# Moving the softmax steps of a fused FFT and soft mixture-of-experts kernel to other places in its written order

## The chip, the cores and the metric

The kernel runs on one core of one Trainium2 chip. The metric is the device time in microseconds (us) of one execution. The engines are named as in the profile: PE (TensorE, matmuls and transposes), PEld (its weight loads), DVE (VectorE), ACT (ScalarE), POOL (GpSimd) and SP (SyncE, which issues all the DMAs here).

## What is computed

The input x is 8 batches of 2496 x 256 float32. The real part of its 2-D Fourier transform, reshaped to 19968 tokens of 256, goes into a soft mixture of experts with 8 experts of 4 slots each:

```python
x = np.fft.fft(np.fft.fft(x, axis=1), axis=2).real.reshape(B * S, D)   # 19968 x 256
logits = x @ phi                                    # 19968 x 32
d = softmax(logits, axis=0)                         # over all tokens
slot_input = (d.T @ x).reshape(8, 4, 256)
slot_out[e] = np.maximum(slot_input[e] @ w1[e], 0.0) @ w2[e]
c = softmax(logits, axis=1)                         # over the 32 slots
out = c @ slot_out                                  # 19968 x 256
```

Both softmaxes subtract the maximum first and add 1e-9 to the sum.

## The kernel before

The 8 batches are worked on as 4 pairs. The transform is never written out: phi is transformed instead, so the first part of the program (parts a to e, d, u) computes the logits of each pair and the sums over tokens. Part m combines the pairs' sums to the experts' input. Parts l and v are the experts: l is h = relu(slot input x w1), in two groups of 32 matmuls (l00, l10), with the relu on ACT (hs) and a transpose on DVE (hT); v is the second matmul (so), also in two groups (v00, v10). Part r copies the experts' output to a replicated matrix rh, by an ACT copy (sos), one matmul (sorep) and two ACT scalings. Everything after this writes the output.

The softmax over slots belongs to each pair and has six steps, named x in the order with the pair and the step:

- x_0, `logits`: 11 transposes of the pair's logits on PE (cT), in groups of 4, 4 and 3, each group copied by ACT to the tile c. The two PSUM banks with the tag p1 are shared by cT and lT.
- x_1, `less_max` for both halves: a max reduce on DVE and a subtraction on POOL each.
- x_2 and x_3, `exp` of one half each, on ACT.
- x_4 and x_5, `over_sum` of one half each: sum reduce, small scaling (adding 1e-9) and reciprocal on DVE, then a multiplication on POOL.

Part s is all six steps of one pair at once. Part k (k00 to k32) transposes a piece of a finished softmax on PE (lT) and copies it with ACT (lTs). Pieces 0, 1 and 2 serve the output blocks 0 and 1, 2 and 3, and 4. Part o is an output block: 8 matmuls as the profile counts them (po, against rh) in two halves, whose banks are emptied by one ACT copy and one DVE copy each (line 612), then a DMA on SP. There are 5 blocks for each of 4 pairs, 20.45 MB in all. Six PSUM banks serve po. The first block of the first pair is sent in three DMAs, the last block of a pair in two pieces.

The order is written by hand: `ORDER` is a list of parts with a pair and an index, and the parts are traced in that order. A planner then orders each engine's queue; it may put work that is ready earlier ahead. `after` holds it back: it queues what a part traces behind the last output matmul and the last output copies traced so far, each on its own engine, with no wait for their end. Where there are none yet, it takes the instruction in `anchor["u"]`, the last matmul of part u. `GATE` holds back the cT groups of pairs 0 and 1 in the same way on PE: for pair 1 behind `anchor["slot"]`, the last matmul of part m. `part_s` also holds its DVE work behind the copies of sT, the experts' input.

In the order before, the first pair's softmax stands between the experts' two groups of h (l00 s00 l10), the second's right after them (s10), ahead of v00. The third's and the fourth's six steps are spread over the output blocks of the first and second pair, from k01 to k11 and from o11 to o21.

Of the kernel before, what the change touches and what calls it, by code (L numbers as in the profile page):

```python
# [15 lines left out]
D = 256  # L16
# [11 lines left out]
SEB = 2  # L28
DE = 2
FIRST = [0, 1]  # L30
GATE = {0: ['u', 'acc', 'acc'], 1: ['slot', 'slot', 'slot']}
P1, P2, P3, PM = 2, 2, 3, 0
W2 = [1, 1, 1, 1, 1, 1, 1, 1, 1, 1, 1, 2, 2, 1]
ORDER = (
# [6 lines left out]
).split()  # L41


# [69 lines left out]
def _build(nc, tc, xh, phih, w1h, w2h, cins, where, out, out0):  # L113
    from contextlib import ExitStack, nullcontext

    v, sc, pe = nc.vector, nc.scalar, nc.tensor
    ctx = ExitStack()
    with ctx:
# [8 lines left out]
        def ring(name):  # L127
            return sb.tile([128, 8, D], F32, name=name, tag="ring", bufs=RING)
# [13 lines left out]
        def bank(name, dt=F32):  # L142
            return pp.tile([128, 512], dt, name=name, tag="ps")
# [31 lines left out]
        def C(name):  # L175
            i, o, r, w = where[name]
            return cs[i][:r, o : o + w]
# [5 lines left out]
        ps = bank("psphi")  # L183
# [238 lines left out]
        acc = cp.tile([128, 129], F32, name="acc")  # L422
        at = cp.tile([128, 64], F32, name="at")
        sT = cp.tile([128, 2, NSLOT], F32, name="sT")
        anchor = {}
# [79 lines left out]
        def part_r():  # L505
            so = sos_[0]

            rh.append(sb.tile([128, 2, D], F32, name="rh", tag="d", bufs=2))
            sos = sb.tile([128, D], F32, name="sos", tag="dpm", bufs=2)
            ps = bank("sorep")  # L510
            sc.copy(sos, so[:, :D])
            pe.matmul(ps[:, :D], C("sel2"), sos, start=True, stop=True)
            for k in range(2):
                sc.activation(rh[0][:, k], ps[:, :D], AF.Copy, scale=C("turn")[:, k : k + 1])  # L514
            banks.close()
            pool_o.append(ctx.enter_context(tc.tile_pool(name="po", bufs=6, space=PSUM)))
# [4 lines left out]
        def logits(p):  # L521
            L = lt[p]
            cq[p] = sb.tile([128, 40, NSLOT], F32, name=f"c{p}", tag=CT[p], bufs=bufs_(CT[p]))
            for b in range(3):
                ps = bank1(f"cT{p}_{b}")
                n = min(4, NG - 4 * b)
                with tc.issue_after(anchor[GATE[p][b]]) if p in GATE else nullcontext():
                    for j in range(n):
# [50 lines left out]
        behind, lts = {}, {}  # L579
# [12 lines left out]
            for t in range(n):  # L592
                lts[p, 2 * j + t // 2, t % 2] = lT[:, t]

        def part_o(p, b):
            ot = ring(f"o{p}_{b}")
            done = 0
            for t in range(2):

                po = [pool_o[0].tile([128, 512], F32, name=f"po{p}_{b}_{2 * t + h}", tag="po") for h in range(2)]  # L600
                for h in range(2):
                    rows = slice(64 * h, 64 * h + 64)
                    with tc.issue_after(behind["pe"]) if "pe" in behind else nullcontext():
                        ins = pe.matmul(  # L604
                            po[h], lts[p, b, t][rows], rh[0][rows].rearrange("p k d -> p (k d)"),
                            start=True, stop=True, tile_position=(64 * h, 0),
                        )
                    behind["pe"] = ins.ins
                for h, ev in ((0, sc.copy), (1, v.tensor_copy)):
                    i = 2 * t + h  # L610
                    np_ = 64 if b == 4 and i == 3 else 128
                    ins = ev(ot[:np_, 2 * i : 2 * i + 2, :].rearrange("p k d -> p (k d)"), po[h][:np_])  # L612
                    behind[h] = ins.ins
                    if b == 4 and i == 3:
                        nc.sync.dma_start(out0[p].rearrange("p (r d) -> p r d", d=D), ot[:64, 6:8])
                    elif i == 3 or (b == 4 and i == 2) or ((p, b) == (0, 0) and i in FIRST):
                        nc.sync.dma_start(
                            out[p, :, (8 * b + done) * D : (8 * b + 2 * i + 2) * D].rearrange("p (r d) -> p r d", d=D),
                            ot[:, done : 2 * i + 2],
                        )  # L620
                        done = 2 * i + 2

        def after(f, *a):

            with ExitStack() as order:
                for ins in behind.values() if behind else [anchor["u"]]:
                    order.enter_context(tc.issue_after(ins))
                f(*a)

# [2 lines left out]
            "e": part_e, "d": part_d, "u": lambda p, _: part_u(p), "w": lambda *_: load_w(),  # L632
            "m": lambda *_: part_m(), "l": lambda i, _: part_l(i), "v": lambda i, _: part_v(i),
            "r": lambda *_: part_r(), "s": lambda p, _: after(part_s, p), "x": lambda p, i: after(part_x, p, i),
            "k": lambda p, j: after(part_k, p, j), "o": part_o,
        }
        for what in ORDER:
            parts[what[0]](int(what[1]), int(what[2]))
# [50 lines left out]
```

## Time and profile before

| | |
|---|---|
| median of 3 runs | 198.22 us (197.83 to 199.21) |
| the profiled execution | 199.02 us |
| its span | 196.9 us |
| PE busy | 170.5 us, 87% of the span |
| DVE busy | 125.4 us, 64% |
| ACT busy | 111.2 us, 56% |
| POOL busy | 20.8 us, 11% |
| granted TensorE clock, mean | 0.982 |
| moved by DMA | 38.46 MB read, 20.45 MB written |

The profile shows one execution. The page gives each engine's busy time and cuts the span into 40 slices. Other views of the same trace are windows (busy time of each engine in a stretch, the number of instructions in brackets, then the granted clock, the share of time in which the 16 DMA engines were busy, and GB/s), the timeline of one engine (start, length, instruction, and in brackets the idle time before it and what ended that), and the chain of waits, which is followed back from the last instruction. The operands in a row are written out<-in by the program's names.

### The profile page before, as it was taken

To read this page: it belongs to the slowest core of one execution; us is meant where nothing else is said; L and a number is where in the kernel's file an instruction comes from. 1 tells how busy PE (TensorE), PEld (TensorE's weight loads), DVE (VectorE), ACT (ScalarE), POOL (GpSimd) and SP (SyncE) were. 2 spreads that over 40 slices of the span, in tenths; PEclk is the share of its full clock that TensorE was granted. 3 is DMA by queue.
4 is the path that set the end of the run, shared out by engine and by line. 5 is a ranking of instruction groups with operands and counts; after the bars stand their busy time and mean duration, and the time that the engine had idled before them with its cause. 6 is when DMAs were issued, how large, how long until landed. Compare 5 with 4: busy or idle time off the path is not lost.

```text
span 196.9 us, 4194 instructions
## 1 busy us (share of the span) xinstructions
PE 170.5 (87%) x1682; PEld 106.8 (54%) x1682; DVE 125.4 (64%) x227; ACT 111.2 (56%) x244; POOL 20.8 (11%) x25
## 2 busy tenths in 40 slices
PE   0489899899999989999998999997999999999500
PEld 0466586586777857577855876253443443344100
DVE  0699877999995972712475644980376887965500
ACT  2133586578964684675844725542659759676400
POOL 0000000000000000000000004482022522500000
PEclk9999999999999999999999999999999999999975
DMA  5999999999960699303921989940468999999993
GB/s 182 417 426 408 421 415 424 421 415 399 361 245 0 208 421 423 119 0 113 320 107 17 343 260 396 415 180 0 164 267 343 364 426 416 385 426 381 418 423 149
DMA packets 10706, 59.16 MB, mean 300 GB/s; under 512 B 1344, under 2 KB 1728, under 8 KB 5696
## 3 DMA queue, kind: packets, MB, share of 16 engines
q1 hardware_dynamic: 10688, 58.91, 76.1%
q8 instruction: 13, 0.21, 0.4%
q14 instruction: 5, 0.04, 0.0%
HBM read 38.46 MB, written 20.45 MB: 299 GB/s over the span
## 4 chain that ended last, share of the span: by engine, by line
PE 79%; DVE 6%; ACT 4%; DMA 2%; issue 2%; POOL 1%; SPq 0%; ACTq 0%; DVEq 0%
PE po L604 18%; PE pt L229 10%; PE z L244 8%; PE e L335 6%; PE d L353 5%; PE a L279 5%; PE u L376 4%; PE h L477 4%; PE so L497 4%; PE cT L529 3%; PE lp L297 2%; DMA x<-xh 2%; PE lT L588 2%; PE lm L298 2%; PE zt L265 2%; ACT et L230 2%
## 5 line engine op out<-in xcount | busy, mean ns | idle before, releaser
L604 PE MATMUL po<-rh,lTs 64*128 64x512 f32 x160 | 38.7, 610 | 1.6 <-ACT rh L514 0.9
L612 DVE COPY o<-po 128x512 f32<-128x512 f32 (+1 forms) x40 | 27.0, 683 | 17.5 <-PE po L604 16.8
L229 PE MATMUL pt<-cs,eo 128*128 128x128 f32 x160 | 26.2, 301 | 7.7 <-DVE eo L224 7.6
L230 ACT COPY et<-pt 128x512 f32<-128x512 f32 x40 | 22.8, 587 | 14.8 <-PE pt L229 14.7
L612 ACT COPY o<-po 128x512 f32<-128x512 f32 x40 | 23.3, 586 | 12.1 <-PE po L604 12.1
L229 PEld LDWEIGHTS pt<-cs,eo 128*128 128x128 f32 x160 | 19.8, 153 | 14.2 <-DVE eo L224 7.6
L604 PEld LDWEIGHTS po<-rh,lTs 64*128 64x128 f32 x160 | 14.2, 186 | 16.4 <-issue 11.3
L222 DVE TENSOR_TENSOR x<-x 128x1024 f32<-128x1024 f32 x16 | 19.4, 1214 | 3.1 <-DMA x<-xh 3.1
L244 PE MATMUL z<-et,wphi 128*32 128x256 f32 (+1 forms) x288 | 16.8, 368 | 2.4 <-ACT et L230 2.4
L546 POOL TENSOR_TENSOR c<-c,cm 128x640 f32<-128x640 f32 x8 | 9.9, 1264 | 66.8 <-DVE cm L545 66.8
L320 ACT ACTIVATE d<-lt,nm 120x128 f32<-120x128 f32 x44 | 13.7, 392 | 3.6 <-DVE nm L317 3.6
L335 PE MATMUL e<-cs,dpm 120*64 120x120 f32 x176 | 14.0, 273 | 0.0
L224 DVE TENSOR_TENSOR eo<-x 128x512 f32<-128x512 f32 x20 | 13.7, 682 | 0.3
L225 DVE TENSOR_TENSOR eo<-x 128x512 f32<-128x512 f32 x20 | 13.6, 679 | 0.0
L244 PEld LDWEIGHTS z<-et,wphi 128*32 128x32 f32 x288 | 8.1, 114 | 9.3 <-ACT et L230 3.9
L279 PE MATMUL a<-cs,zt 128*120 128x128 f32 x88 | 11.8, 279 | 1.0 <-DVE lt L302 0.9
L335 PEld LDWEIGHTS e<-cs,dpm 120*64 120x64 f32 x176 | 11.4, 136 | 2.4 <-issue 1.8
L252 ACT COPY zs<-z 128x512 f32<-128x512 f32 (+1 forms) x12 | 6.2, 513 | 10.4 <-PE z L244 10.4
L376 PE MATMUL u<-eo,ds 128*32 128x129 f32 x320 | 11.5, 275 | 0.1
L556 POOL TENSOR_TENSOR c<-c,cm 128x640 f32<-128x640 f32 x8 | 10.1, 1264 | 13.1 <-DVE cm L555 13.1
L279 PEld LDWEIGHTS a<-cs,zt 128*120 128x120 f32 x88 | 10.4, 183 | 2.1 <-DVE lt L302 1.1
L353 PE MATMUL d<-e,cs 128*64 128x320 f32 x64 | 10.7, 443 | 0.5 <-ACT ds L359 0.5
(91 smaller groups left out, 215.9 us busy)
## 6 DMA issues: line engine op xcount, KB each, us to landing
x<-xh SPq DMA_DIRECT2D x16, 1024.0 KB, 12.2
out<-o SPq DMA_DIRECT2D x15, 1024.0 KB, 6.3
w<-w1h SPq DMA_DIRECT2D x6, 1024.0 KB, 8.1
w<-w2h SPq DMA_DIRECT2D x12, 512.0 KB, 6.3
x<-xh SPq DMA_DIRECT2D x4, 896.0 KB, 11.9
out<-o SPq DMA_DIRECT2D x4, 768.0 KB, 6.2
w<-w1h SPq DMA_DIRECT2D x4, 512.0 KB, 5.5
w<-w2h SPq DMA_DIRECT2D x2, 1024.0 KB, 7.2
```

Source lines behind the costliest of these rows:

```text
L222: v.tensor_tensor(x[:, 0:4], x[:, 0:4], x[:, 4:8], op=ALU.add)
L224: v.tensor_tensor(e[:, :, 0:128], x[:, 0:4, 0:128], x[:, 0:4, 128:256], op=ALU.add)
L229: pe.transpose(b[:, g * 128 : g * 128 + 128], e[:, g, k * 128 : k * 128 + 128], ident)
L230: sc.copy(tr[k][:, :, :, qi, :], b.rearrange("p (g h a) -> p g h a", g=4, h=2))
L244: pe.matmul(z[32 * g : 32 * g + 32, o : o + n], wphi[:, w, :], tr[k][:, g].rearrange("p h q a -> p (h q a)"), start=w != 0, stop=w != 1, t ...
L279: pe.matmul(ps[:120, i * 128 : i * 128 + 128], zt[p][:, GS * g : GS * g + GS].rearrange("p s h c -> p (s h c)"), C("wa"), start=True, stop ...
L320: sc.activation(d[:, g], L[:, g], AF.Exp, bias=nm[:, g : g + 1], scale=1.0)
L335: pe.matmul(ps[64 * k : 64 * k + 64, 120 * i : 120 * i + 120], dpm[p, hf][:, k, 3 * j + i, :], C(name), start=True, stop=True, tile_positi ...
L353: pe.matmul(ps[64 * h : 64 * h + 64, :320], C("wb")[:, 64 * k : 64 * k + 64], esb[p].rearrange("p g (s h c) -> p (g s) h c", h=2, c=NKC)[: ...
L376: last = pe.matmul(ub[32 * g : 32 * g + 32, 0:129], dsb[p][:, k, c, :], e[:, 0:129] if k == 0 else e[:, 127:256], start=cc == 0, stop=cc == 9,
L604: ins = pe.matmul(po[h], lts[p, b, t][rows], rh[0][rows].rearrange("p k d -> p (k d)"), start=True, stop=True, tile_position=(64 * h, 0),)
L612: ins = ev(ot[:np_, 2 * i : 2 * i + 2, :].rearrange("p k d -> p (k d)"), po[h][:np_])
```

## The change

The order of the parts is written anew from m00 on, and four small pieces of code go with it.

- s10 is gone. In its place the second pair's six steps stand behind r00 as x10 to x15, spread over the first pair's output blocks.
- The third pair's steps begin after block 3 of the first pair (x20) and are spread over the second pair's blocks; the fourth's are spread over the third's in the same way.
- k00 stands ahead of r00 rather than behind it.
- Block 3 of the first three pairs is traced in two halves, g and h, with the fifth step of a softmax between them. `part_o` keeps its tile and its count of sent columns in a dictionary for that.
- The three cT groups of pair 1 are held behind a new anchor "rep", the matmul sorep of part r.
- `after` takes the last matmul of v10, if traced, as long as no output block is there.

```diff
-GATE = {0: ['u', 'acc', 'acc'], 1: ['slot', 'slot', 'slot']}
+GATE = {0: ['u', 'acc', 'acc'], 1: ['rep', 'rep', 'rep']}
...
-    "u30 m00 l00 s00 l10 s10 v00 v10 r00 k00 o00 k01 x20 o01 x21 o02 k02 x22 o03 "
-    "k10 x23 o04 x24 o10 k11 x25 o11 x30 o12 k12 x31 o13 k20 x32 o14 x33 o20 k21 "
-    "x34 o21 x35 o22 k22 o23 k30 o24 o30 k31 o31 o32 k32 o33 o34"
+    "u30 m00 l00 s00 l10 v00 v10 k00 r00 x10 o00 x11 k01 o01 o02 x12 x13 k02 g03 x14 h03 x15 x20 "
+    "o04 k10 o10 x21 k11 o11 x22 x23 o12 k12 g13 x24 h13 x25 x30 o14 k20 o20 x31 k21 o21 x32 x33 "
+    "o22 k22 g23 x34 h23 x35 o24 k30 o30 k31 o31 o32 k32 o33 o34"
...
-            pe.matmul(ps[:, :D], C("sel2"), sos, start=True, stop=True)
+            ins = pe.matmul(ps[:, :D], C("sel2"), sos, start=True, stop=True)
+            anchor["rep"] = ins.ins
...
-        def part_o(p, b):
-            ot = ring(f"o{p}_{b}")
-            done = 0
-            for t in range(2):
+        ots = {}
+
+        def part_o(p, b, ts=(0, 1)):
+            for t in ts:
+                if t == 0:
+                    ots[p, b] = ring(f"o{p}_{b}"), 0
+                ot, done = ots[p, b]
...
                         done = 2 * i + 2
+                ots[p, b] = ot, done
...
-                for ins in behind.values() if behind else [anchor["u"]]:
+                for ins in behind.values() if behind else [anchor.get("v1", anchor["u"])]:
...
+            "g": lambda p, b: part_o(p, b, (0,)), "h": lambda p, b: part_o(p, b, (1,)),
```

## The prediction

> **What bounds the kernel now.** I read the page's forty slices first, then the windows of the second half, then the chain of waits, then the queues of ACT, DVE and POOL around the moved steps. The page:
> ```profile
> span 196.9 us, 4194 instructions
> PE 170.5 (87%) x1682; PEld 106.8 (54%) x1682; DVE 125.4 (64%) x227; ACT 111.2 (56%) x244; POOL 20.8 (11%) x25
> DMA  5999999999960699303921989940468999999993
> HBM read 38.46 MB, written 20.45 MB: 299 GB/s over the span
> ```
> TensorE has the most work, but it does not set the end. In the last third of the DMA line the digits are 9 up to the last slice. Windows of that stretch (engines, granted clock, then DMA share and GB/s):
> ```profile
> 139.00:140.00 1.00, 1.00 (x6) 0.19 (x2) 0.61 (x1) 0.58 (x1) 0.00 (x0) 1.00 0.06 16
> 143.00:144.00 1.00, 1.00 (x8) 0.68 (x8) 0.69 (x1) 0.93 (x2) 0.00 (x0) 1.00 0.41 156
> 144.00:145.00 1.00, 1.00 (x7) 0.30 (x3) 0.27 (x1) 0.51 (x2) 0.00 (x0) 1.00 0.31 131
> 147.00:148.00 1.00, 1.00 (x8) 0.47 (x6) 1.00 (x3) 0.10 (x1) 1.00 (x2) 1.00 0.11 41
> 148.00:149.00 1.00, 1.00 (x8) 0.42 (x4) 0.91 (x2) 1.00 (x2) 1.00 (x1) 1.00 0.31 131
> 193.00:194.00 1.00, 0.00 (x0) 0.00 (x0) 0.00 (x0) 0.00 (x0) 0.00 (x0) 0.50 0.68 244
> 139.90:194.20 54.30, 44.29 (x212) 19.47 (x210) 33.81 (x56) 32.56 (x60) 10.03 (x8) 0.96 0.93 376
> 148.70:194.20 45.50, 35.49 (x169) 15.43 (x167) 27.95 (x47) 26.92 (x50) 7.93 (x7) 0.95 1.00 402
> ```
> Output transfers begin at about 139.9, need 54.30 x 0.93 = 50.5 us of transfer in all (12.6 a pair), and have no gap after 148.7. Their gaps lie earlier: 143.4 to 144.7, between the first pair's first block (o00) and o01, and 147.1 to 148.7, between o01 and o02. So two things set the end: when the first output matmul starts, and how soon the queue of outputs is never empty again. The way to the first output matmul is on the chain (start, length, what):
> ```profile
> 119.83 0.85 PE cT L529 x8
> 120.68 3.57 PE h L477 x32
> 124.25 0.46 PE cT L529 x3
> 124.75 3.64 PE h L477 x32
> 128.38 0.59 PE lT L588 x4
> 128.97 7.09 PE so L497 x128
> 136.08 0.38 ACT sos L511
> 136.51 0.71 PE sorep L512 x2
> 138.14 1.99 PE po L604 x8
> ```
> The cT there are the second pair's logits, 0.85 + 0.46 us of TensorE between the experts' matmuls; the first pair's lT also stands ahead of so.
>
> **The change, stage 1: up to the first output matmul.** No arithmetic and no DMA is added: the same 26 output DMAs leave SP in the same order, since the split of block 3 into two calls issues them at the same half. Moved past the experts are, of the second pair, 11 cT transposes on PE, 3 copies on ACT, 2 + 2 reduces, 2 scalings and 2 reciprocals on DVE, 4 POOL operations and 2 exponentials. k00's four transposes (lT) now queue behind the last so matmul.
>
> The experts can then start when sT is copied, not when cT is through:
> ```profile
> 119.64 0.41 DVE L459 COPY sT<-slotin 128x32 f32<-128x32 f32 x2 [1.03 <-PE slotin L457]
> 123.38 0.74 ACT L549 ACTIVATE c<-c 128x640 f32<-128x640 f32 x1 [0.48 <-POOL c L546]
> 124.02 1.25 ACT L485 ACTIVATE hs<-h,sm 128x512 f32<-128x512 f32 x2
> ```
> The first of the two copies ends near 119.85, so h starts at about 119.95 in place of 120.68: 0.73 of the 0.85 is gained. The cT of 0.46 goes too, and some 0.07 of waits is left. lT leaves its place ahead of so (0.59), and comes back where PE now waits 0.43 for ACT's sos (136.08 to 136.51): 0.16 of it shows. By steps: 119.95 + 3.6 + 3.7 = 127.25, so to 134.35, lT to 134.94, sorep 0.71, then the 0.92 to po that are there now (137.22 to 138.14): 136.6, **1.55 us earlier**. In those 0.92 us PE stands idle today, and the second pair's first eight cT (0.85) fit there at no cost; the last three (0.46) fall into the first block.
>
> One step of this hangs on ACT's order. The second group of h waits for a bank that hs frees, and hs ran at 124.02, behind two exponentials of the first pair, although its h was ready near 122.5 (half of 3.64 after 120.68). If the queue keeps that order, h's second group starts at 124.75 as now, and only 0.59 - 0.16 = 0.43 is gained. With h ready at 121.8 it is earlier than the second exponential could start (123.38), and hs stands ahead of it in the written order; I take 1.55. The experts' last weights must not be late then:
> ```profile
> 131.00:132.00 1.00, 1.00 (x28) 0.57 (x21) 1.00 (x3) 0.00 (x0) 0.69 (x1) 1.00 0.02 8
> ```
> No transfer is left after 131.0, and the last quarter of so would start at 134.35 - 1.8 = 132.5, so they are not.
>
> **Stage 2: from the first output matmul (T) to the end.** Before, T is 138.14; transfers end near 193.9, T + 55.8. The gap before o02 came from DVE:
> ```profile
> 139.39 1.49 DVE L612 COPY o<-po 128x512 f32<-128x512 f32 x2 [6.47 <-PE po L604]
> 143.12 0.69 DVE L612 COPY o<-po 128x512 f32<-128x512 f32 x1 [0.17 <-PE po L604]
> 145.71 1.55 DVE L545 TENSOR_REDUCE cm<-c 128x20 f32<-128x640 f32 x2 [0.28 <-ACT c L534]
> 147.17 2.06 DVE L612 COPY o<-po 128x512 f32<-128x512 f32 x3
> ```
> Two reduces of the third pair's softmax stood ahead of o02's last copy, which ended at 147.86. In the changed order the two reduces of that stretch (the second pair's) are traced behind o00, whose last copy ends at T + 2.74, and are over at T + 4.3; o01's two copies end at T + 5.7 to 6.1 (before: 143.81, T + 5.67), and o02 meets no reduce. So o01 is later by 0.2 (middle of 0 and 0.4) and the 1.6 us gap goes: at most 1.4 gained.
>
> Against this, the cover that hid the softmaxes is gone. Before, the third pair's was computed a whole pair ahead of its use, the fourth's nearly so; now each is made within the five blocks before its use. What that makes of one pair's length:
> ```profile
> 149.44 3.70 PE po L604 x16
> 163.90 1.99 PE po L604 x8
> 153.58 1.26 POOL L556 TENSOR_TENSOR c<-c,cm 128x640 f32<-128x640 f32 x1 [4.48 <-DVE cm L555]
> 160.44 1.55 DVE L545 TENSOR_REDUCE cm<-c 128x20 f32<-128x640 f32 x2 [0.28 <-ACT c L534]
> 168.04 1.26 POOL L556 TENSOR_TENSOR c<-c,cm 128x640 f32<-128x640 f32 x1 [4.22 <-DVE cm L555]
> 140.75 0.58 ACT L591 COPY lTs<-lT 128x512 f32<-128x512 f32 x1
> ```
> The 16 at 149.44 are o04 and o10, so o10 starts near 151.3, and the 8 at 163.90 are o20: a pair with another's softmax beside it took 13.15 and 12.6 us. From first reduce to the end of the first half's last POOL step the softmax took 145.71 to 154.84 = 9.1 and 160.44 to 169.30 = 8.9, to which lT (0.66 or less, 0.59 on the chain) and its copy (0.58) add 1.2: 10.2. In the new order the reduce comes 2.7 after a pair's first matmul (as o00's above) and the next pair can't start before 2.7 + 10.2 = **12.9**. TensorE's own work for a pair is less: 40 po at 3.70 / 16 = 9.25, lT 0.59 + 0.59 + 0.37, cT 1.31, together 12.1. Fourth pair's first block out: three such pairs, 2.7 to its last copy, 0.9 from copy to transfer (143.81 to 144.7), then 12.6 of transfer: T + 3 x 12.9 + 16.2 = T + 54.9. That is **0.85 less** than T + 55.8 and lies above the other bound (T + 54.4), so it counts. The ends: 1.4 gained if the latency hides better, 0 at a pair of 13.2 (39.6 + 16.2 = 55.8), a loss beyond.
>
> One place where DVE and POOL meet is dearer in the changed order:
> ```profile
> L554 DVE TENSOR_SCALAR cm<-cm x8: 176/176/825, 123.8 to 169.9; 128x20 f32<-128x20 f32 x8
> 129.55 1.27 POOL L556 TENSOR_TENSOR c<-c,cm 128x640 f32<-128x640 f32 x1
> 130.03 0.82 DVE L554 TENSOR_SCALAR cm<-cm 128x20 f32<-128x20 f32 x1
> ```
> The small scaling takes 176 ns, but 825 when it began under a POOL operation, and ended with it; the copies of 147.17, under POOL too, took their usual 0.69. That is 0.65 for each meeting, which today happens only between the experts; in the new order it can come once a pair, behind the first half's last POOL step. By my slots the second half's scaling starts after POOL is done, so I put it at zero, and keep 3 x 0.65 = 1.95 as its upper end. The Trainium skill, "SBUF — State Buffer", "Who interferes with whom", says that such DVE operations and GpSimd exclude each other for a whole instruction, and that PSUM copies with one SBUF side don't; the trace agrees (825 against 176 ns, and 0.69). Counted as the page allows it, at every pair, the sum would be 1.95 higher.
>
> **The sum.** -1.55 - 0.85 = -2.4 us. The profiled execution took 199.02 with 2.1 outside its 196.9 span, so its like would take 196.6; it stood 0.8 above the median of 198.22, which gives **195.8 us**.
>
> **The rivals.** *ACT's order stays.* hs remains behind both exponentials: stage 1 gives 0.43, the sum is -1.3, 196.9 us. For it: the planner chose that order once. Against it: h is ready 0.7 earlier, and hs is written first.
> *The pairs don't get shorter.* At 13.2 a pair stage 2 gives nothing: 198.2 - 1.55 = 196.7. For it: exponentials stand ahead of o12's and o22's copies on ACT (0.74 each), and the waits of 4.48 and 4.22 before POOL show how loosely these steps ran; against it, in the third pair's 10.9 us, with half of a softmax in them, DVE and ACT are busy 8.68 and 8.14, so there is room:
> ```profile
> 163.90:174.80 10.90, 10.90 (x52) 4.88 (x54) 8.68 (x16) 8.14 (x15) 2.53 (x2) 1.00 1.01 406
> ```
> *Slower: the softmax's latency becomes the bound.* One place: lT of the next pair's first block, waiting for POOL. Every us that the softmax takes beyond 10.2 is paid three times, since no later pair has spare transfers queued. It costs all of stage 1 at a pair of 13.2 + 1.55 / 3 = 13.7, a latency of 11.0, and 1% (2 us) at 14.4. With one POOL operation (1.26) and one blocked scaling (0.65) more it is 12.1: pairs of 14.8, 3 x 1.6 - 1.55 = +3.3, 201.5 us. Against it: the bare steps are reduce 0.8, POOL 1.26, exponential 0.74, reduce 0.8, scaling and reciprocal 0.5, POOL 1.26, lT and copy 1.2, together 6.6, so 3.6 of the 10.2 is queueing already.
>
> **How the numbers follow.** About 1%, 2 us, is what a measurement can tell from no change. Forecast 0.62; ACT's order stays 0.17; pairs not shorter 0.12; latency 0.09. The forecast's own range is 194.8 (stage 2 at its end of 1.4, and 0.5 for the spread of the runs) to 196.8; 0.50 of its 0.62 is under 196.2 and 0.12 above. Of the second, 0.02 is faster; the rest of it and the third are within 1%; the fourth is slower. Faster 0.52, same 0.39, slower 0.09. The range goes to 198.5, which holds the second and third rivals with some of the blocked scalings (196.7 + 1.8), and leaves out the fourth and a little at the bottom.
>
> **What would show it.** Stage 1: no cT between the two groups of h on the chain, hs ahead of the second exponential, first po near 136.6. Stage 2: no window of DMA share under 0.9 between o01's transfer and the end; po of o10, o20 and o30 about 12.9 apart; L554 at 176 ns. Wrong if: h's second group still starts at 124.75; idle TensorE ahead of k10, k20 and k30, released by POOL L556; or DMA windows with gaps behind 150.

## The result, and the profile after

Six runs of each kernel gave 195.56 us for the changed kernel (194.77 to 195.88) and 198.51 for the one before (196.84 to 199.79): a ratio of 0.9859, with a 95% interval from 0.9812 to 0.9907. In two later rounds, on two chips, the ratio was 0.9797 (0.9764 to 0.9831) and 0.9817 (0.9766 to 0.9867). So it is faster by 1.4 to 2%, or 2.9 to 3.9 us, where 2.4 were forecast. Ratios here and below leave out runs over 1.5% longer than the fastest of their kernel, while the times given are medians of all runs.

The page after:
```profile
span 193.0 us, 4197 instructions
PE 169.5 (88%) x1682; PEld 107.7 (56%) x1682; DVE 125.2 (65%) x227; ACT 111.0 (58%) x244; POOL 20.9 (11%) x25
DMA  5999999999980399600860689990279999999995
```
The engines run the same numbers of these instructions as before, and their busy times differ by at most 1.0 us, so the gain is not less work. The profiled execution took 194.9. Its chain of waits, from the experts on (start, length, what):
```profile
119.75 3.64 PE h L477 x32
123.39 1.92 PE h L477 x16
...
133.96 0.59 PE lT L589 x4
134.55 0.60 PE sorep L512 x2
135.14 0.02 issue
135.17 0.85 ACT rh L515 x2
136.01 0.04 issue
136.06 2.85 PE po L608 x12
...
149.32 1.99 PE po L608 x8
...
162.33 1.99 PE po L608 x8
...
174.83 1.99 PE po L608 x8
```
No cT stands between the groups of h, and the first output matmul is at 136.06 for 138.14. The part ahead of it was 0.14 earlier in this execution (the first pair's seven cT at 118.00 for 118.14), so 1.94 belong to the change. The last three po rows are o10, o20 and o30: pairs of 13.26, 13.01 and 12.50 us.

The transfers, in windows as before:
```profile
141.00:142.00 1.00, 1.00 (x8) 0.39 (x4) 1.00 (x3) 0.73 (x2) 1.00 (x1) 1.00 0.43 168
142.00:143.00 1.00, 1.00 (x8) 0.33 (x6) 0.97 (x3) 0.73 (x2) 1.00 (x2) 1.00 0.19 82
143.00:144.00 1.00, 1.00 (x6) 0.53 (x8) 0.34 (x1) 1.00 (x3) 0.27 (x1) 1.00 1.02 434
165.00:166.00 1.00, 1.00 (x6) 0.52 (x8) 1.00 (x3) 0.59 (x2) 0.11 (x1) 1.00 0.57 168
190.00:191.00 1.00, 0.00 (x0) 0.00 (x0) 0.00 (x0) 0.00 (x0) 0.00 (x0) 0.50 0.94 320
191.00:192.00 1.00, 0.00 (x0) 0.00 (x0) 0.00 (x0) 0.00 (x0) 0.00 (x0) 0.50 0.08 27
```
The gap between o00 and o01 is still there (by the trace's DMA packets nothing moves from 141.6 to 142.9), the one between o01 and o02 is gone. Then there are only partial gaps, the largest at 165. The last transfers end near 191.5. In the kernel before they fade out more slowly than the prediction had read them (the last row here is a quarter of a microsecond):
```profile
194.00:195.00 1.00, 0.00 (x0) 0.00 (x0) 0.00 (x0) 0.00 (x0) 0.00 (x0) 0.50 0.27 82
195.00:196.00 1.00, 0.00 (x0) 0.00 (x0) 0.00 (x0) 0.00 (x0) 0.00 (x0) 0.50 0.03 10
195.25:195.50 0.25, 0.00 (x0) 0.00 (x0) 0.00 (x0) 0.00 (x0) 0.00 (x0) 0.50 0.04 16
```
They end near 195.5, not 193.9; the share is a mean over 16 DMA engines, so a small one can mean that a few still work. From the first output matmul to the last transfer it is 57.4 us before and 55.5 after. So the span's 3.9 us divide into 0.14 of drift, 1.94 ahead of the output and 1.9 behind its start, where 0.85 was forecast.

### The profile page after: what moved, and what is told of

It is laid out like the page before. It is cut to its first block, busy times and chain, and to the rows that moved or that the text cites. A ratio compares the mean times of both kernels' runs of the same rounds, so it can differ in the third digit from the quotient of the medians.

```text
span 193.0 us, 4197 instructions
## 1 busy us (share of the span) xinstructions
PE 169.5 (88%) x1682; PEld 107.7 (56%) x1682; DVE 125.2 (65%) x227; ACT 111.0 (58%) x244; POOL 20.9 (11%) x25
## 4 chain that ended last, share of the span: by engine, by line
PE 79%; DVE 7%; ACT 5%; DMA 3%; issue 1%; POOL 1%; SPq 0%; ACTq 0%; DVEq 0%; POOLq 0%
PE po L608 18%; PE pt L229 10%; PE z L244 8%; PE e L335 7%; PE d L353 5%; PE a L279 5%; PE u L376 4%; PE h L477 4%; PE so L497 4%; PE lT L589 3%; DMA x<-xh 3%; PE lp L297 2%; PE lm L298 2%; PE cT L530 2%; PE zt L265 2%; ACT et L230 2%
## 5 line engine op out<-in xcount | busy, mean ns | idle before, releaser
L608 PE MATMUL po<-rh,lTs 64*128 64x512 f32 x160 | 38.1, 607 | 2.2 <-ACT lTs L592 2.1
L608 PEld LDWEIGHTS po<-rh,lTs 64*128 64x128 f32 x160 | 14.3, 186 | 17.0 <-issue 10.2
L222 DVE TENSOR_TENSOR x<-x 128x1024 f32<-128x1024 f32 x16 | 19.4, 1217 | 2.9 <-DMA x<-xh 2.9
## 6 DMA issues: line engine op xcount, KB each, us to landing
x<-xh SPq DMA_DIRECT2D x16, 1024.0 KB, 12.2
```

What stands on the lines that cost most here:

```text
L222: v.tensor_tensor(x[:, 0:4], x[:, 0:4], x[:, 4:8], op=ALU.add)
L608: ins = pe.matmul(po[h], lts[p, b, t][rows], rh[0][rows].rearrange("p k d -> p (k d)"), start=True, stop=True, tile_position=(64 * h, 0),)
```

## The experiments

All are read against the kernel before, timed on the same chip. T is the first output matmul of the profile, behind the start of the first pair's seven cT (118.07 in the kernel before by PE's timeline, so 20.07 there; 117.93 in the changed kernel, so 18.13).

| kernel | time, us | before, us | ratio (95%) | T |
|---|---|---|---|---|
| changed | 194.32 | 198.25 | 0.9797 (0.9764 to 0.9831) | 18.13 |
| changed, again | 194.56 | 198.37 | 0.9817 (0.9766 to 0.9867) | 18.13 |
| k00 moved alone (e7) | 197.88 | 198.25 | 0.9977 (0.9955 to 1.0) | 19.34 |
| second pair back (e1) | 195.34 | 198.67 | 0.9831 (0.9769 to 0.9892) | 19.35 |
| the same, five rounds | 195.35 | 198.25 | 0.9845 (0.9815 to 0.9876) | 19.35 |
| and the third's reduces back (e12) | 197.01 | 198.93 | 0.991 (0.9885 to 0.9934) | 19.35 |
| second pair moved alone (e2) | 202.42 | 198.67 | 1.0216 (1.0157 to 1.0274) | 18.13 |
| hs behind both exponentials (e3) | 196.75 | 198.67 | 0.9926 (0.9881 to 0.9972) | 19.35 |
| one more POOL operation (e4) | 199.5 | 198.67 | 1.0013 (0.9977 to 1.0048) | 18.13 |
| sums and lT earlier (e9) | 194.54 | 198.25 | 0.981 (0.9781 to 0.9839) | 18.13 |
| and reduces behind o01 (e8) | 195.16 | 198.37 | 0.9838 (0.9798 to 0.9877) | 18.12 |
| and k01 behind o01 (e11) | 195.82 | 198.37 | 0.9871 (0.9828 to 0.9914) | 18.13 |

**The parts of the change.** First the second pair's softmax was put back among the experts, with everything else new.
```diff
-    "u30 m00 l00 s00 l10 v00 v10 k00 r00 x10 o00 x11 k01 o01 o02 x12 x13 k02 g03 x14 h03 x15 x20 "
+    "u30 m00 l00 s00 l10 s10 v00 v10 k00 r00 o00 k01 o01 o02 k02 o03 x20 "
-GATE = {..., 1: ['rep', 'rep', 'rep']}
+GATE = {..., 1: ['slot', 'slot', 'slot']}
```


> Base is the changed kernel (195.56 us; first output matmul at 136.06, end of transfers near 191.1), with the second pair's whole softmax back among the experts (s10, its logits gated as before) and the rest of the new order kept. Theory (both stages count: the start of the output moves the end one for one, and the order behind it sets how often the output queue is empty): first output matmul at 138.0 to 138.3, 2 us later; but the first pair's blocks then carry no reduces, o01 is out near 5.2 after the start instead of 6.7, so about 1.2 comes back: 0.8 slower than the changed kernel, 196.4. Rival 'only the start counts': 2.0 slower, 197.6. Rival 'only the gaps behind the start count': 0.5 to 1.2 faster than the changed kernel, 194.4 to 195.1.

This first measurement could not tell it from the changed kernel (195.34, interval of the ratio 1.2% wide), and its profiled execution had reached the seven cT 0.8 us earlier. So it was run again beside the changed kernel, in more rounds.

> The changed kernel itself, timed beside the other three on one chip: 195.3 to 195.8, first output matmul 18.1 after the first pair's seven cT, by every theory.

> The kernel with the second pair's softmax back among the experts and the rest new, timed beside the changed kernel. Its first look had the first output matmul 1.22 later against the first pair's seven cT (19.28 for 18.06) and a first pair 0.3 shorter. Theory (the start counts one for one, the shorter first pair gives a part back): 0.6 to 1.0 slower than the changed kernel. Rival (the queue of outputs is fed by the third's and fourth's later place alone, and the second pair's move is free of effect): within 0.3 of it.

The changed kernel itself came out at 194.32, below what was expected. The kernel with the second pair back was 1.03 slower; the two intervals of the ratio overlap a little, so the times alone are weak evidence. The profiles agree with them: from the seven cT to the last transfer it is 73.6 us in the changed kernel (117.93 to 191.5) and 74.6 here (117.59 to 192.2). T was 1.22 later. The first rival's 2.0 came from taking all of stage 1 for the second pair's move, but k00's part of it stays in this kernel, which the first expectation had overlooked. That part was then tried on the kernel before.
```diff
-  ... v10 r00 k00 o00 ...
+  ... v10 k00 r00 o00 ...
-                for ins in behind.values() if behind else [anchor["u"]]:
+                for ins in behind.values() if behind else [anchor.get("v1", anchor["u"]) if f is part_k else anchor["u"]]:
```


> The kernel before with one edit: k00's transposes queue behind the last so matmul, ahead of sorep. Theory (they hide in the wait for ACT's sos, and the start counts one for one): first output matmul 0.55 to 0.7 earlier (20.0 to 19.3 behind the first pair's seven cT), the end as much: 197.9 to 198.1 where the kernel before has 198.5. Rival (the gap before o02, which DVE sets, or the clock takes it back): no change, 198.5.

T came 0.73 earlier, the time 0.37, with an interval that reaches to no change. Side by side, then: k00 about 0.4, the second pair's move 1.0, and what lies between e7 and the kernel with the second pair back, the third's and fourth's later place (with block 3 in two halves), 197.88 - 195.35 = 2.5. The part forecast to cost a cover is the largest gain.

**The second pair moved alone**, the third's and fourth's steps where they were:
```diff
-    "u30 ... k00 r00 x10 o00 x11 k01 o01 o02 x12 x13 k02 g03 x14 h03 x15 x20 "
-    "o04 k10 o10 x21 k11 o11 x22 x23 o12 ...
+    "u30 ... k00 r00 x10 o00 x11 k01 x20 o01 x21 o02 x12 x13 k02 x22 g03 x14 h03 x15 "
+    "x23 o04 x24 k10 o10 k11 x25 o11 x30 o12 k12 x31 o13 k20 x32 o14 x33 o20 k21 "
+    "x34 o21 x35 o22 k22 o23 k30 o24 o30 k31 o31 o32 k32 o33 o34"
```


> Only the second pair's softmax is moved behind the experts; the third's and the fourth's steps stand where they were. Theory: first output matmul at 136.1 as in the changed kernel, but two softmaxes share the first pair's blocks on DVE (its 10 copies at 0.69, one softmax at about 4.1, most of another at 3 to 4: 14 to 15 us, against 12.6 of transfers), so o10 starts 14 to 15.5 after the start instead of 13.3, the transfers have gaps there, and 1 to 2 us of the gain are lost: 196.6 to 197.6. Rival 'only the start counts': like the changed kernel, 195.6.

T is as early as in the changed kernel, yet the kernel is 3.75 us slower than the kernel before. "Only the start counts" is out. The loss is larger than the theory's, and PE's timeline and the windows (2 us each) say why:
```profile
152.56 0.66 PE L589 MATMUL lT<-cs,c 128*128 128x128 f32 x4 [2.88 <-POOL c L557]
153.89 3.52 PE L608 MATMUL po<-rh,lTs 64*128 64x512 f32 x8 [0.68 <-ACT lTs L592]
```
```profile
150.00:152.00 2.00, 0.00 (x0) 0.00 (x0) 2.00 (x5) 1.52 (x3) 1.61 (x2) 1.00 0.47 197
154.00:156.00 2.00, 2.00 (x6) 0.97 (x8) 0.56 (x3) 0.00 (x1) 1.42 (x2) 0.50 0.97 364
156.00:158.00 2.00, 2.00 (x10) 0.59 (x8) 1.20 (x2) 1.14 (x2) 0.03 (x1) 0.74 0.03 9
```
DVE is full from 150 to 152 (2.00 of 2.00), TensorE waits 2.88 for the second pair's softmax, then runs o10 at a granted clock of 0.50: 3.52 for eight po that take 1.99 elsewhere. The transfers stop altogether from 149.2 to 151.2 and from 156.2 to 159.1, and for 0.2 and 0.6 more at 164 and 167.

**The ACT order**, by tracing s00 ahead of l00 and holding hs back:
```diff
-    "u30 m00 l00 s00 l10 v00 ...
+    "u30 m00 s00 l00 l10 v00 ...
-            sc.activation(half(p, i), half(p, i), AF.Exp)
+            anchor[f"exp{p}{i}"] = sc.activation(half(p, i), half(p, i), AF.Exp).ins
-                    sc.activation(hs, ps, AF.Relu, scale=mask)
+                    with tc.issue_after(anchor["exp01"]):
+                        sc.activation(hs, ps, AF.Relu, scale=mask)
```


> The changed kernel with the experts' first relu copies (hs) queued on ACT behind both exponentials of the first pair, as ACT had them in the kernel before. Theory (stage 1 hung on that order): the second group of h starts at 124.6 instead of 123.4, the first output matmul at 137.2 to 137.4, and the end moves by the same 1.1 to 1.3: 196.7 to 196.9. Rival 'the experts' matmuls have other work to fill the wait, or the drain of the outputs absorbs it': less than 0.4 later, 195.6 to 196.0.

In the changed kernel's ACT timeline hs stands ahead of the second exponential; in e3's PE timeline the second group of h waits for it:
```profile
122.67 0.67 ACT L485 ACTIVATE hs<-h,sm 128x512 f32<-128x512 f32 x1
123.25 0.74 ACT L550 ACTIVATE c<-c 128x640 f32<-128x640 f32 x1
```
```profile
123.61 3.64 PE L477 MATMUL h<-w,sT 128*32 128x512 f32 x32 [1.23 <-ACT hs L486]
```
T is 1.22 later, as expected. The time (196.75) lies in the expected range, but proves less than T: the runs range from 195.5 to 199.0, and beside the later 194.3 of the changed kernel it would be 2.4 us, not 1.2. In its profile the planner had also put one copy ahead of a reciprocal in the third pair, where TensorE's clock fell, which costs time of its own (below); its slowest runs, at a mean granted clock of 0.985 to 0.986, are not explained by that.

**The softmax's latency**, with one more POOL operation:
```diff
+            if p and i == 0:
+                x2 = sb.tile([128, 20, NSLOT], F32, name=f"twice{p}", tag="twice", bufs=1)
+                nc.gpsimd.tensor_tensor(x2, c, m.unsqueeze(2).to_broadcast([128, 20, NSLOT]), op=ALU.mult)
             nc.gpsimd.tensor_tensor(c, c, m.unsqueeze(2).to_broadcast([128, 20, NSLOT]), op=ALU.mult)
```


> The changed kernel with one more POOL operation (the same multiplication into a scratch tile, 1.26 us) ahead of the first half's last one, for pairs 2 to 4. Theory (the softmax's latency sets the length of the first three pairs, 13.26, 13.01 and 12.50 us now): each is 1.2 longer, about 14.3, 14.2 and 13.8, the start is unchanged at 136.1, and the end is 3 to 3.8 later less nothing, since no transfers are queued: 198.5 to 199.3. Rival 'the transfers set the end and the latency has slack': pairs grow by less than 0.5, or the queue absorbs it, and the time stays under 196.5.

The ratio is 1.0013 where the changed kernel had 0.98 to 0.986: some 3 to 4 us lost, as the theory said. The first pair grew from 13.26 to 14.57 (o10 at 150.59 behind 136.02), all of the 1.26. So the latency had no slack there. In the profiled execution (202.26 us) TensorE's clock fell as well, to 0.50 at 154 and at 183; but four runs with a mean granted clock of 0.993 or 0.994 still took 198.2 to 198.7, so the loss does not hang on that. That a pair's length also sets the end was not shown by this, since here the transfers stopped as well (from 153.5 to 155.1 for the first time behind o01). The next kernel turns it round:
```diff
-    "... x12 x13 k02 g03 x14 h03 x15 x20 "
-    "o04 k10 o10 x21 ... k12 g13 x24 h13 x25 x30 o14 k20 o20 x31 ...
-    "o22 k22 g23 x34 h23 x35 o24 k30 o30 ...
+    "... x12 x13 k02 x14 o03 x15 k10 "
+    "o04 x20 o10 x21 ... k12 x24 o13 x25 k20 o14 x30 o20 x31 ...
+    "o22 k22 x34 o23 x35 k30 o24 o30 ...
```


> The changed kernel with the fifth step of each softmax ahead of block 3, the next pair's first lT traced ahead of block 4 and its logits behind block 4. Two claims on a pair's length of 12.9 are set apart. If the softmax's latency sets it, or the wait of 0.7 from the next pair's lT through ACT's copy to its first po, which this order fills with cT: pairs of 12.2 to 12.4, no idle TensorE between pairs, and the three gaps of transfers behind 150 (0.19, 0.43 and 0.15) go: 194.7 to 195.1 for 195.6. If TensorE's own work or the copies set it: pairs stay at 12.8 to 13.2 and the time at 195.6.

The chain of e9 shows o10, o20 and o30, and the windows its transfers:
```profile
135.46 2.85 PE po L608 x12
...
148.21 2.78 PE po L608 x12
...
160.87 2.78 PE po L608 x12
...
172.89 1.99 PE po L608 x8
```
```profile
141.00:142.00 1.00, 1.00 (x7) 0.24 (x4) 1.00 (x2) 0.58 (x1) 1.00 (x2) 1.00 0.00 0
142.00:143.00 1.00, 1.00 (x6) 0.60 (x8) 0.71 (x2) 0.99 (x2) 0.66 (x1) 1.00 0.78 328
190.00:191.00 1.00, 0.00 (x0) 0.00 (x0) 0.00 (x0) 0.00 (x0) 0.00 (x0) 0.50 0.39 121
191.00:192.00 1.00, 0.00 (x0) 0.00 (x0) 0.00 (x0) 0.00 (x0) 0.00 (x0) 0.50 0.01 4
```
The pairs are 12.7, 12.7 and 12.0, 1.3 us less in all (12.2 to 12.4 were expected), and all partial gaps behind 150 but one of 0.1 are gone. The time stayed (194.54 beside 194.32). The expectation had the time follow the pairs' length, and it did not. In both kernels transfers start again with o01, 6.9 behind the first output matmul, and end 48.6 to 48.8 after that.

**Can o01 come earlier?** Two more orders tried it, both built on e9's.
```diff
-    ... x10 o00 x11 k01 o01 o02 ...
+    ... x10 o00 k01 o01 x11 o02 ...     (e8)
+    ... x10 o00 o01 x11 k01 o02 ...     (e11)
```


> The changed kernel again as the measure for the next two: 194.3 to 195.6.

> The order of e9 with the second pair's two reduces traced behind o01 instead of o00. With pairs at 12.7 and 12.1 e9 was no faster, so the theory is now: the output transfers set the end, which is the moment o01 is out plus the rest of the transfers, 55 behind the first output matmul; the pairs' length has slack. Then o01's last DVE copy, which stood behind the reduces (140.74 to 141.4 in e9), comes 0.4 to 0.5 earlier, the gap of transfers between o00 and o01 shrinks from 1.4 to about 1.0, and the time falls by 0.4 to 0.5 against e9 and the changed kernel. Rival (the pairs' length or the latency of the softmax sets the end): the reduces are 1 later, so no gain or a loss of up to 1.

> As e8, with k01's transposes and copy behind o01 too, so that o01's second half follows its first but for three cT. Theory (o01's moment sets the end): o01 out 0.8 to 0.9 earlier than in e9, the gap between o00 and o01 down to 0.5 or 0.6, the end 0.8 to 0.9 earlier: 193.5 to 194.0 where the changed kernel has 194.3 to 194.9. Rival: no gain, since o02 and the softmax are later.

Neither gained; the rival was right about the outcome. The gap between o00 and o01 shrank, from 1.4 us in e9 (140.9 to 142.3) to 0.6 in e8 (142.6 to 143.2) and 0.3 in e11 (141.9 to 142.2), and o01's transfer starts 6.9, 6.5 and 6.0 behind the first output matmul. But the softmax was later, so that the first pair grew to 13.3 and 13.8 (o10's po at 150.05 behind 136.72, and 149.95 behind 136.17), and the transfers stopped later instead, in both for the last time ahead of o11. The row of e8:
```profile
156.00:157.00 1.00, 1.00 (x8) 0.34 (x6) 1.00 (x3) 0.86 (x2) 1.00 (x2) 1.00 0.26 107
```
At this order several limits lie close together, and moving one brought up the next. No kernel tried is clearly better than the changed one.

**The decisive step by itself.** The kernel with the second pair back got the third pair's first two steps (the logits, and the two reduces with their subtractions on POOL) back into the first pair's blocks, and nothing else.
```diff
-    "u30 ... s10 v00 v10 k00 r00 o00 k01 o01 o02 k02 o03 x20 "
-    "o04 k10 o10 x21 k11 ...
+    "u30 ... s10 v00 v10 k00 r00 o00 k01 x20 o01 x21 o02 k02 o03 "
+    "o04 k10 o10 k11 ...
```


> The kernel with the second pair's softmax among the experts and the third's and fourth's later (0.9845 of the kernel before), with one thing put back: the third pair's logits and its two reduces stand in the first pair's blocks as in the kernel before (behind k01 and o01), the rest of its softmax stays late. Theory now (the end is the moment at which the queue of outputs is last wholly empty, plus what is left at the pace of the slowest DMA engine, 0.39 to 0.4 MB a us, so that a gap before o02 is paid once in full and no later slack helps): the two reduces stand ahead of o02's last copy again, the transfers stop for 1.2 to 1.6 between o01 and o02, and the time is 1.3 to 2.2 above that kernel: a ratio of 0.991 to 0.996, 196.7 to 197.5. Rival (a pair's length, or the latency of the softmax, sets the end: pair 2 now has slack of 12 us in its softmax and can only be shorter): 0.980 to 0.985.

The DVE timeline and the windows of e12:
```profile
144.23 1.54 DVE L546 TENSOR_REDUCE cm<-c 128x20 f32<-128x640 f32 x2 [0.28 <-ACT c L535]
145.69 2.06 DVE L616 COPY o<-po 128x512 f32<-128x512 f32 x3
```
```profile
145.00:146.00 1.00, 1.00 (x8) 0.35 (x6) 1.00 (x3) 0.73 (x2) 0.88 (x1) 1.00 0.65 262
146.00:147.00 1.00, 1.00 (x6) 0.53 (x8) 0.97 (x2) 0.45 (x2) 1.00 (x2) 1.00 0.02 8
193.00:194.00 1.00, 0.00 (x0) 0.00 (x0) 0.00 (x0) 0.00 (x0) 0.00 (x0) 0.50 0.07 27
```
The two reduces stand ahead of o02's last copy, no transfer runs from 146.1 to 147.3, and the ratio goes from 0.9845 to 0.991: 1.3 us, at the lower end of what was expected. The two rounds ran on different chips, each beside the kernel before, and their intervals (up to 0.9876, and from 0.9885) do not meet. The rival's 0.980 to 0.985 is out. From the first output matmul to the last transfer it is 55.3 us in the kernel with the second pair back, 56.9 in e12 and 57.1 in e7. So in the profiles these two steps account for nearly all that the later place gains; in the timed runs for 1.3 of 2.5, and the other 1.2 stay unexplained. The first pair is 0.34 longer than without the reduces (o10 at 149.96 behind 136.66, and 149.90 behind 136.94), the other two are the same (13.01 and 12.50 for 13.00 and 12.50).

## Why the prediction was right, and where its steps were not

**Stage 1** was right in mechanism and mis-sized by 0.4 (1.55 forecast, 1.94 measured). The second pair's move gave 1.22 of it, by the terms as forecast (0.73 + 0.46). hs ran ahead of the second exponential, as assumed, and e3 priced that at 1.22. The term that was off is k00: its transposes were to show 0.16 behind so, a gain of 0.43, and it gained 0.72. Behind so the transposes end at 134.55 and sorep starts there, in the place where it would have waited for sos and its issue; next to nothing of them shows. That a shift of T moves the end about one for one is borne out by the second pair's move (1.22 of T, 1.03 of time, 1.0 in the profiles); for k00 (0.73 of T in e7) the 0.37 is too near the noise to say, but in the profiles the last transfer came 1.0 earlier behind the seven cT (76.4 for 77.4).

**Stage 2** came out at the forecast pair length and for another reason. The three pairs took 38.8 us, 12.9 each, as written. But the wait in the first two is not for POOL: lT follows the last cT without a pause, and TensorE then waits 0.67 and 0.73 for ACT's copy of it, in PE's timeline of the changed kernel. Only the third pair waits for POOL:
```profile
149.32 1.99 PE L608 MATMUL po<-rh,lTs 64*128 64x512 f32 x8 [0.67 <-ACT lTs L592]
162.33 1.99 PE L608 MATMUL po<-rh,lTs 64*128 64x512 f32 x8 [0.73 <-ACT lTs L592]
173.44 0.66 PE L589 MATMUL lT<-cs,c 128*128 128x128 f32 x4 [0.90 <-POOL c L557]
```
The softmax's latency stood level with these: POOL had ended 0.16 and 0.62 before those two lT began, and e4, e8 and e11 made the first pair longer at once. That the sum of 2.7 and 10.2 came out is partly luck. From the first reduce to the end of the first half's last POOL step a softmax took 8.0 to 8.4, where the prediction had 8.9 to 9.1; and in the first pair the reduces began 3.82 behind T, not 2.7.

The step that failed is "it counts": of the two bounds on the end, the prediction let the pairs' length decide (0.85) over the vanished gap (1.4). It rests on a misreading. The prediction took the end of the transfers before as 193.9, where the share falls, and not as 195.5, where it becomes zero, so that the end was T + 55.8 for it and not T + 57.4. Read rightly, the bound of the gap is T + 56.0 (57.4 less 1.4), which lies above the T + 54.9 of the pairs, and by the prediction's own rule the gap would have decided. (The transfers also begin at 140.8, not 139.9, on which the sum does not rest.)

The runs say the same. By e9 the pairs may be 1.3 shorter in all with no effect, and by e12 the gap alone is worth 1.3. What fits all of these is that the end is the moment at which transfers are last stopped altogether, plus the rest at a pace of 0.39 to 0.40 MB a microsecond. Before, that moment is 148.7 (o02), and 46.8 us follow for 18.35 MB; in e7 it is 147.0 and 46.5 follow, in e12 147.3 and 46.3. Where the last stop is the one ahead of o01, one block more is left: 48.6 us for 19.4 MB in the changed kernel (from 142.9) and 48.8 in e9 (from 142.3). Ahead of o11, with 14.3 MB left, 36.1 us follow in e8 (from 157.0) and in e11 (from 156.9). The rows of e7:
```profile
146.00:147.00 1.00, 1.00 (x7) 0.33 (x4) 0.91 (x3) 0.82 (x2) 1.00 (x2) 1.00 0.00 0
193.25:193.50 0.25, 0.00 (x0) 0.00 (x0) 0.00 (x0) 0.00 (x0) 0.00 (x0) 0.50 0.07 25
```
At that pace a pair's 5.11 MB take about 12.9 us (an estimate from these figures; the prediction had 12.6; with 12.9 the bound of the pairs is T + 55.2, still under the gap's). The changed kernel's pairs are 12.9 long in the mean, so shorter ones, as in e9, had nothing to win, and e4's longer first one let the transfers run dry.

Of the 1.9 gained behind T, the stop that went is 1.2 (147.5 to 148.7), and o01's later start took 0.3 back. The remaining 0.9 or so is that the transfers from o01 on, that stop left out, took 48.6 us in the changed kernel and 49.6 before. In e7, e12, the kernel with the second pair back and e9 they took 49.3, 49.1, 49.1 and 48.8, one execution each. Why the kernel before is the slowest of these was not shown.

Two of the prediction's signs of being wrong did appear, and cost little: a wait for POOL ahead of k30 (0.90), and partial gaps behind 150, the largest with a share of 0.57. Both terms of the sum came out too small (1.55 for 1.94, 0.85 for 1.9), and the later rounds' 194.32 and 194.56 lie just below the forecast's lower end of 194.8.

The reduces stood in the queue where forecast, behind o00, but began 1.1 later than written, after a wait for ACT's copy of the logits. They still ended early enough for o01's last copy to end 5.97 behind the first output matmul (141.34 and 0.69 for one copy), inside the forecast 5.7 to 6.1.
```profile
139.88 1.54 DVE L546 TENSOR_REDUCE cm<-c 128x20 f32<-128x640 f32 x2 [0.21 <-ACT c L535]
141.34 2.00 DVE L616 COPY o<-po 128x512 f32<-128x512 f32 x3
```
The small scaling met POOL in one pair of the three and took 0.72 in place of 0.18 there, 0.54 more on DVE. Put at zero, it was not zero; that pair's next lT had no wait for POOL, so it was not seen to cost time:
```profile
146.63 1.26 POOL L557 TENSOR_TENSOR c<-c,cm 128x640 f32<-128x640 f32 x1 [3.36 <-ACT c L535]
147.20 0.72 DVE L555 TENSOR_SCALAR cm<-cm 128x20 f32<-128x20 f32 x1
```

**The rivals.** ACT's order did not stay. The pairs did get shorter than 13.2 in the mean; what three pairs of 13.2 would have cost was not tried, but e8 and e11, with a first pair of 13.3 and 13.8, had a full stop ahead of o11. The slower case, the latency of the softmax, was the one nearest: e4 with 1.26 more gave back all of the gain, against a forecast break-even at 0.8 more.

## What to carry to other kernels

Where a queue of outputs drains at the end, find the last moment at which it stood still, and what the block that ended that pause was waiting for; here only work ahead of that block, or a later pause, moved the end. Read the end of the queue where its share becomes zero, not where it falls. The softmax steps were cheap beside this drain as long as none of them stood ahead of the first blocks' copies on the same engine, and as long as TensorE did not run dry over them. Before working on a stage's length, compare it with the pace of the drain, shorten it once by an order that costs nothing, and see if the time follows.

## What the runs showed of the hardware that was not expected

**A drain without pauses ends raggedly.** The end was looked at in windows of 0.25 us, from the last one with a share over 0.85 to the last with any transfer. That took 2.25 us in the kernel before and in e7, and 1.75 in e12, whose transfers had not stood still for some 44 us by then. It took 1.25 in e9 and 0.5 in the changed kernel, where it is 48 us since the last full stop, but 35 and 22 since the last window of 1 us with a share of 0.9 or less (39 in the kernel before, by that count). In the changed kernel timed again (its second profile), with a full stop at 182, it was also 0.5. So, with partial gaps counted, the tail is some 2 to 6% of the time since the last gap, as if the 16 engines ran at slightly different paces and partial gaps were the quicker ones waiting. The views give no reading of a single DMA engine, so the cause stays open; if it is so, it would explain why the partial gaps of the changed kernel cost nothing that e9 could win.

**TensorE's clock fell after short waits, in some executions only.** The changed kernel waits at the end of the third pair, from about 172.5 to 174.8 with one lT in between. In the first profile the next eight po took 1.99. In the two later ones they took 3.38 and 3.00, because the granted clock fell to 0.50, for some 3.4 us. The rows of the last:
```profile
174.56 3.00 PE L608 MATMUL po<-rh,lTs 64*128 64x512 f32 x8 [0.73 <-ACT lTs L592]
```
```profile
176.00:177.00 1.00, 1.00 (x4) 0.00 (x0) 0.61 (x1) 0.46 (x1) 0.00 (x0) 0.50 0.98 412
178.00:179.00 1.00, 1.00 (x5) 0.61 (x5) 0.31 (x1) 0.47 (x2) 0.00 (x0) 0.60 0.36 107
```
The transfers then ran dry at 178, and that execution took 195.72, where two others of the same kernel took 193.5 and 193.6. The clock is not the whole spread: another took 196.04 at a mean granted clock of 0.989. The Trainium skill, "TensorE: Matmul & The Clock Gate", "What's actually happening", says that the clock is halved after an idle window of about 3.4 us which runs free of the kernel, so that where it changes varies from run to run. The halving, the variation and the 3.4 us for which it lasted agree; the idle time ahead of it does not, since here a stretch of 2.3 us with 0.66 us of transposes in it was enough.
